# Attention with a fourth buffer for the stacks of keys, loads spread over the head steps, and a background list paced at 1.2 parts a step

## The chip, the cores and the metric

One core of a Trainium2 chip. The time is that of one execution on the device in microseconds (us); with one core its span is the program's. TensorE (PE) multiplies into PSUM, VectorE (DVE), ScalarE (ACT) and GpSimd (POOL) work on the results, and SyncE (SP) does nothing but issue transfers (DMAs). Every engine runs its own instructions in the order in which they were written, and waits at an instruction until what it depends on has been done.

## The reference

Two independent parts share the program. Part A is attention with 32 heads of 18 dimensions over a sequence of 2048, cut into 4 groups of 512 positions:

```python
for s in range(N):                       # N = 4 groups of L = 512 positions
    qs, ks, vs = q[:, :, s], k[:, :, s], v[:, :, s]
    p = softmax(einsum("bhqd,bhkd->bhqk", qs, ks) * scale + mask)   # causal inside the group
    a_dot = einsum("bhqk,bhkd->bhqd", p, vs)
    pq = phi(qs)                                                     # t+1 above zero, exp(t) below
    num = einsum("bhld,bhde->bhle", pq, M)
    den = einsum("bhld,bhd->bhl", pq, z)[..., None] + 1e-6
    outs.append(g * num / den + (1.0 - g) * a_dot)
    M = M + einsum("bhld,bhle->bhde", phi(ks), vs)
    z = z + einsum("bhld->bhd", phi(ks))
return (outs, heads side by side) @ wo
```

`M` and `z` are the memory of all earlier groups and `g` is a gate for each head. Part B multiplies the two-dimensional Fourier transform of another input of 2048 x 576 by given weights and transforms back.

## The kernel before

The program runs in four stages: forward transform of part B (to about 80 us), the projections q, k and v of part A with the middle of the transform beside them (to 287 us), the inverse transform with the first scores of attention beside it (to 377 us), and attention (377 to 882 us). The whole order is written out by hand: nothing is moved by a scheduler, so the order of the text is each engine's order. The change is in `ATT`, in what is issued from the third stage on.

**Stacks.** A stack is 8 heads of one group, so there are 16 (n = 0 to 15), 4 for each group. `stack_dmas` (L579) loads a stack's queries into `Qs[n%3]` and its keys into `Ks[n%3]` with six transfers each from `qkD` in device memory (three parts of bfloat16, stacked along the partitions in the pairs that the product needs), all issued by SP at L588; `load_v` (L594) brings the values. Rows 108 and 109 of a `Qs` hold the row maxima that `mpath` puts there; the same rows of a `Ks` hold -1.

**Head steps.** `attention` (L806) runs t = 0 to 132. A step's main work is `s1(t+10)`, the scores of a head ten steps on, of which DVE takes the row maxima (L603, L607; three parts); `s2(t)`, the scores of head t with the maxima taken off, ACT's exponentials and, every fourth head, POOL's four masks (L641 to L657; three parts); and `pv` (L668), the products with the values of four heads, one quarter a step. Every fourth step `mpath` turns the maxima of four heads (L622 on PE, L626 and L627 on ACT, L630 on DVE) and two transfers from POOL, `put(0)` and `put(1)` (L624), place them in `Qs`. `s1` of stack n starts at t = 8n-10.

**Queues.** At t = 8n the thirteen issues of stack n+2 are put on the list `q`. Two are taken in the middle of each step and up to two at its end, where the list `qu` (the results `U` of a stack, written back to `uD` and `rD`) comes first.

**Background list.** `bg` holds generators whose parts are run at the end of the steps, 1.6 parts a step on average (`run_bg(1.6)`, L864): `late_setup` (weights of the output product), and for each group `combine` (adds the memory's share to the attention), five `mem1` (the memory's numerators of the next group), `den` (its denominators) and `oproj` (the output product). They use one PSUM buffer, tag `post`: a product there can start only when the one before has been read out. The `lane` holds short chains such as `recip`, which advance once a step. `ln` starts at step 10 of a group (of 32 steps), and after `recip` it loads `ux` three times, waits three steps and hands `combine`, `mem1`, `den` and `oproj` to `bg`. In `mem1` the product `pn` (L735) and its copy `am` (L739) lie in two parts; in `oproj` the copy of one half of a block stands behind the first five products of the next half in the order of the text (`pend`), and each half of 15 products is three parts.

**Prologue.** During the inverse transform `prologue` loads stacks 0 and 1 and runs `s1` of the first ten heads.

Of the kernel before, what the change touches and what calls it, by code (L numbers as in the profile page):

```python
# [5 lines left out]
F32=mybir.dt.float32; F32R=mybir.dt.float32r  # L6
# [361 lines left out]
class ATT:  # L368
# [174 lines left out]
    def att_setup(s,cp):  # L543
        nc,io=s.nc,s.io
        s.Qs=[];s.Ks=[]
        for i in range(3):
            q=cp.tile([128,8,512],BF,name=f"Qs{i}"); k=cp.tile([128,8,512],BF,name=f"Ks{i}")
            s.Qs.append(q); s.Ks.append(k)
        for i in range(3): nc.gpsimd.dma_start(s.Ks[i][108:110].rearrange("p h c -> p (h c)"),io["neg1"])
        s.mask=cp.tile([128,512],F32,name="mask"); nc.sync.dma_start(s.mask,io["mask"])  # L550
        bt=cp.tile([128,1],F32,name="bt"); nc.sync.dma_start(bt,io["beta"])
        e=cp.tile([128,1],F32,name="be"); s.gt=cp.tile([128,1],F32,name="gt"); s.g1=cp.tile([128,1],F32,name="g1")
        nc.scalar.activation(e,bt,AF.Exp,scale=-1.0)
        nc.vector.tensor_scalar(e,e,1.0,None,op0=OP.add)
        nc.vector.reciprocal(s.gt,e)
        nc.vector.tensor_scalar(s.g1,s.gt,-1.0,1.0,op0=OP.mult,op1=OP.add)
        d=lambda n,sh,dt: s.dp.tile(sh,dt,name=n)
        s.uD=[d(f"uD{i}",[576,512],F32) for i in range(4)]
        s.rD=[d(f"rD{i}",[32,512],F32) for i in range(4)]
        s.dD=[None]+[d(f"dD{i}",[32,512],F32) for i in range(1,4)]  # L560
        s.rrD=[d(f"rrD{i}",[64,512],F32) for i in range(4)]
        s.rdD=[None]+[d(f"rdD{i}",[64,512],F32) for i in range(1,4)]

    def late_setup(s,cp):
# [13 lines left out]
        yield  # L578
    def stack_dmas(s,n):  # L579

        nc=s.nc; g,G=divmod(n,4)
        Q,K=s.Qs[n%3],s.Ks[n%3]
        L=[]
        for (T,base,order) in ((Q,0,(0,0,0,1,1,2)),(K,576,(0,1,2,0,1,0))):
            for pc,o in enumerate(order):
                a=s.qkD[g][base+8*G*18:base+8*G*18+18,o]
                ap=bass.AP(tensor=a.tensor,offset=a.offset,ap=[[1536,18],[1536*18,8],[1,512]])
                L.append(lambda T=T,pc=pc,ap=ap: nc.sync.dma_start(T[18*pc:18*pc+18],ap))  # L588
        L.append(lambda: s.loaded.add(n))
        return L  # L590
# [5 lines left out]
    def s1(s,t):  # L596

        nc=s.nc; k,hh=divmod(t,4); n,qd=divmod(k,2); h=4*qd+hh
        Q,K=s.Qs[n%3],s.Ks[n%3]; tp=s.sm
        assert n in s.loaded,(t,n)  # L600
        if hh==0: s.mg[k]=tp.tile([128,4,4],F32,name="mg")
        def mm(out,i):
            nc.tensor.matmul(out,Q[:108,h,128*i:128*i+128],K[:108,h,:128*(i+1)],start=True,stop=True)  # L603
        def red(src,i):
            w=128*(i+1)
            junk=tp.tile([128,512],BF,name="junk",bufs=2)
            nc.vector.tensor_tensor_reduce(out=junk[:,:w],in0=src,in1=s.mask[:,512-w:],scale=1.0,scalar=-3.0e38,  # L607
                op0=OP.add,op1=OP.max,accum_out=s.mg[k][:,hh,i:i+1])
        pa=s.ps1.tile([128,512],F32,name="s1",tag="s1")
        mm(pa[:,:128],0); mm(pa[:,128:],2); red(pa[:,:128],0); red(pa[:,128:],2)  # L610
        yield
        pc=s.ps1.tile([128,512],F32,name="s1",tag="s1")
        mm(pc,3); red(pc,3)
        yield
        pb=s.ps1.tile([128,256],F32,name="s1",tag="s1")
        mm(pb,1); red(pb,1)
        yield
    def mpath(s,k):
# [3 lines left out]
        nc.tensor.transpose(pt,s.mg.pop(k).rearrange("p h i -> p (h i)"),s.ident)  # L622
        mt=s.sm.tile([16,2,128],BF,name="mts")
        def put(a): nc.gpsimd.dma_start(Q[108+a:109+a,4*qd:4*qd+4].rearrange("p h (i c) -> p (h i) c",c=128),mt[:,a])  # L624
        mf=s.sm.tile([16,128],F32,name="mf")
        nc.scalar.copy(mf,pt)  # L626
# [6 lines left out]
    def s2(s,t):  # L633
        nc=s.nc; k,hh=divmod(t,4); n,qd=divmod(k,2); h=4*qd+hh
        Q,K=s.Qs[n%3],s.Ks[n%3]; tp=s.tp
        if hh==0: s.P[k]=[tp.tile([128,4,w],F32,name=f"P{i}") for i,w in enumerate((512,512,256))]
# [49 lines left out]
    def recip(s,src,dst,gate,eps,load):  # L686
        nc=s.nc; tp=s.tp
        x=tp.tile([128,128],F32,name="rx")
        nc.sync.dma_start(x,src.rearrange("h (b c) -> (h b) c",b=4))
# [3 lines left out]
        if eps: nc.vector.tensor_scalar(x,x,1e-6,None,op0=OP.add)  # L693
        y=tp.tile([128,128],F32,name="ry")
        nc.vector.reciprocal(y,x)
        nc.vector.tensor_scalar(y,y,gate,None,op0=OP.mult)
        w=tp.tile([128,2,128],F32R,name="rw")
        nc.vector.tensor_copy(w[:,0],y)
# [14 lines left out]
    def den(s,g,lane):  # L713
        nc=s.nc; tp=s.tp
        ds=tp.tile([128,512],F32,name="ds",bufs=1); ds2=tp.tile([32,512],F32,name="ds2",bufs=1)
        for T,d in ((range(4),ds),((4,),ds2)):
            pd=s.ps.tile([128,512],F32,name="pd",tag="post")
            for t in T:
                r=126 if t<4 else 72
                nc.tensor.matmul(pd[32*(t%4):32*(t%4)+32],s.zst[g][:r,t],s.pq[g,t][:r],start=True,stop=True,skip_group_check=True)  # L720
            yield
            nc.scalar.copy(d,pd[:d.shape[0]])
        for t in range(5):
# [8 lines left out]
    def mem1(s,g,t):  # L732
        nc=s.nc; r=126 if t<4 else 72
        pn=s.ps.tile([126,512],F32,name="pn",tag="post")
        nc.tensor.matmul(pn[:r],s.Mst[g][:r,t,:r],s.pq.pop((g,t))[:r],start=True,stop=True)  # L735
        if g<3: s.pq_load(g+1,t)
        yield
        am=s.tp.tile([126,512],F32,name="am",bufs=5)
        nc.scalar.copy(am[:r],pn[:r])  # L739
        pb=s.ps.tile([126,512],F32,name="pb",tag="post")  # L740
# [4 lines left out]
    def ux_load(s,g,t):  # L745
        r=126 if t<4 else 72
        s.ux[t]=s.tp.tile([126,512],F32,name="ux",bufs=3)
        s.nc.sync.dma_start(s.ux[t][:r],s.uD[g][126*t:126*t+r])
    def combine(s,g):

        nc=s.nc; tp=s.tp; xs=s.ux
        s.oh=[None]*5; s.ol=[None]*5
        for t in range(7):
            if t>1:
# [16 lines left out]
    def oproj(s,g):  # L771
        nc=s.nc; pend=None
        oh,ol=s.oh,s.ol
        for tb in range(4):
            ob=s.tp.tile([128,576],F32,name="ob")
            c=slice(128*tb,128*tb+128)
            for hf in range(2):
# [3 lines left out]
                for i,(a,b,t) in enumerate(L):  # L781
                    r=126 if t<4 else 72
                    nc.tensor.matmul(ps,a[t][:r,c],b[:r,t,w],start=i==0,stop=i==14)  # L783
                    if i==4 and pend: pend(); pend=None
                    if i%5==4: yield
                def pend(ob=ob,w=w,ps=ps,hf=hf,tb=tb):
                    nc.scalar.copy(ob[:,w],ps)  # L787
                    if hf==1: nc.sync.dma_start(s.io["ya"][g*512+128*tb:g*512+128*tb+128],ob)
        pend()
        yield  # L790
    def begin(s,sm,sp,ps1):
        s.sm,s.sp,s.ps1=sm,sp,ps1
        s.mg={};s.m2={};s.P={};s.vs={};s.rc={};s.am={};s.pq={};s.ux={};s.loaded=set()
    def prologue(s):

        for n in range(2):
            for i,f in enumerate(s.stack_dmas(n)):
                f()
                if i%4==3: yield
            s.load_v(n)  # L800
        for i in range(4): yield
        for t in range(10):
            yield from s.s1(t)
            if t in (4,8): m=s.mpath(t//4-1); next(m)
            if t in (5,9): next(m)
    def attention(s,tp,ps):  # L806
# [18 lines left out]
        for t in range(133):  # L825
            k,hh=divmod(t,4); n,qd=divmod(k,2); g=k//8
            if k<32 and hh==0 and qd==0 and n+2<16:
                q+=s.stack_dmas(n+2); q.append(lambda n=n: s.load_v(n+2))
            st=t%32
            if 16<=t<21: s.pq_load(1,t-16)  # L830
            if t==34: bg.append(s.den(1,lane))
            if st==10 and g>0:
                def ln(g=g):
                    yield from s.recip(s.rD[g-1],s.rrD[g-1],s.g1,False,"rr")
                    for u in range(3): s.ux_load(g-1,u)
                    for u in range(3): yield
                    bg.append(s.combine(g-1))
# [4 lines left out]
            a=s.s1(t+10) if t+10<128 else iter(())  # L842
            b=s.s2(t) if t<128 else iter(())
            steps(a,1)
            steps(b,1)
            steps(a,1)
            steps(b,1)
            if 4<=t-1<132: s.pv((t-5)//4,(t-5)%4)
            for _ in range(2):
                if q: q.pop(0)()  # L850
            steps(a,1)
            if hh==2 and k+2<32: m=s.mpath(k+2); next(m)
            steps(b,1)
            if hh==3 and m is not None: steps(m,1); m=None
            if t>=8 and t%4==0:
                s.pv_out((t-8)//4)
                if t%8==4: qu+=s.u_dmas((t-12)//8)
            for l in list(lane):
                try: next(l)
                except StopIteration: lane.remove(l)  # L860
            for _ in range(2):
                if qu: qu.pop(0)()
                elif q: q.pop(0)()
            run_bg(1.6)  # L864
        while q: q.pop(0)()
        while qu: qu.pop(0)()
        lane.append(s.recip(s.rD[3],s.rrD[3],s.g1,False,"rr"))
        while lane or bg:
            for l in list(lane):
                try: next(l)  # L870
                except StopIteration: lane.remove(l)
            run_bg(2.0)
        for u in range(3): s.ux_load(3,u)
        for _ in s.combine(3): pass
# [99 lines left out]
```

## Time and profile before

| what | value |
|---|---|
| median of three runs | 881.58 us (879.1 to 884.06) |
| profiled execution | 884.07 us |
| its span | 882.1 us, so 1.97 us lie around it |
| PE busy | 742.6 us (84%) |
| DVE busy | 584.8 us (66%) |
| ACT busy | 466.5 us (53%) |
| POOL busy | 182.5 us (21%) |
| DMA | 121.25 MB, 137 GB/s on the mean |
| granted clock of TensorE | 0.930 on the mean |

A line of the page's fifth part or of the waits names an engine, a line of the kernel and the operation; "idle before" is the time for which the engine stood still just ahead of such an instruction, and the arrow names what ended it. In a list in order of time the first two numbers are start and length in us; a number in brackets at the end is that idle time. "PEclk" is the share of full clock that was granted to TensorE, and "DMA" is the mean busy share of the core's 16 DMA engines.

### The profile page before, as it was taken

The page shows a single profiled execution, that of the slowest core. Times are in us where ns is not written, and L with a number is a line of the kernel's source. Part 1 is how long each engine was busy: PE and PEld are TensorE (multiplying, and loading weights), DVE is VectorE, ACT ScalarE, POOL GpSimd, SP SyncE. Part 2 cuts the span into 40 slices and gives each one's busy share as a digit, 9 for nine tenths or more (in the row PEclk, how much of TensorE's full clock was granted, in tenths as well). Part 3 has the DMA queues.
Part 4 walks back from the last instruction along what each step waited for, and adds up shares of the span by engine and source line. Part 5 has one row for each costly group of instructions (what it writes and reads, how often), then busy time and mean ns, then how long its engine had stood idle before and what let it go on. Part 6 is the DMA issues. An engine that isn't in the chain of part 4 may idle for free.

```text
span 882.1 us, 14645 instructions
## 1 busy us (share of the span) xinstructions
PE 742.6 (84%) x4751; PEld 495.3 (56%) x4751; DVE 584.8 (66%) x1687; ACT 466.5 (53%) x996; POOL 182.5 (21%) x339
## 2 busy tenths in 40 slices
PE   5988999999999699967777885888957798977856
PEld 4887797887979598922333331245512255422646
DVE  5998897977878799656665785546765565861040
ACT  3666966748565344346555664455644455664111
POOL 2110001010011644225332331122311121331000
PEclk9999999999999899978888998989977899989968
DMA  8873546445537685365654664534463345310121
GB/s 286 273 226 106 173 151 210 144 146 175 169 138 254 162 211 165 108 169 117 145 124 97 131 150 110 130 88 110 115 162 79 83 103 141 107 34 15 62 74 54
DMA packets 82463, 121.25 MB, mean 137 GB/s; under 512 B 9338, under 2 KB 49400, under 8 KB 82254
## 3 DMA queue, kind: packets, MB, share of 16 engines
q1 hardware_dynamic: 74836, 104.29, 42.3%
q0 software_dynamic: 7552, 16.03, 6.3%
q8 instruction: 38, 0.62, 0.3%
q14 instruction: 37, 0.30, 0.1%
HBM read 81.72 MB, written 38.35 MB: 136 GB/s over the span
## 4 chain that ended last, share of the span: by engine, by line
PE 57%; DMA 14%; DVE 11%; ACT 11%; issue 5%; POOL 1%; SPq 1%; ACTq 0%; DVEq 0%; POOLq 0%
PE pj L440 9%; PE po L783 8%; PE pv L668 8%; PE s L603 7%; PE pjv L440 7%; DMA Ks<-qkD 3%; DMA Qs<-qkD 3%; PE s L641 2%; DMA ux<-uD 2%; PE i L292 2%; PE i L303 2%; PE s L645 2%; PE pn L735 2%; DMA yb<-yout 2%; PE pm L497 1%
## 5 line engine op out<-in xcount | busy, mean ns | idle before, releaser
L607 DVE CUSTOM_DVE_ANT_0 junk<-s,mask 128x128 bf16<-128x128 f32 (+3 forms) x512 | 225.8, 485 | 118.0 <-PE s L603 116.2
L603 PE MATMUL s<-Ks,Qs 108*128 108x128 bf16 (+3 forms) x512 | 142.4, 323 | 27.4 <-DMA Ks<-qkD 10.5
L642 ACT ACTIVATE P<-s 128x512 f32<-128x512 f32 x128 | 76.4, 597 | 140.8 <-PE s L641 134.0
L603 PEld LDWEIGHTS <-Qs 108*128 108x128 bf16 x512 | 47.2, 102 | 130.0 <-issue 115.9
L668 PE MATMUL pv<-P,vs 128*32 128x512 f32 (+3 forms) x1024 | 104.8, 484 | 1.6 <-issue 1.1
L653 POOL TENSOR_SCALAR_AFFINE_SELECT P<-P 128x512 f32<-128x512 f32 x128 | 81.0, 663 | 50.9 <-ACT P L642 49.3
L624 POOL DMA_DIRECT2D Qs<-mts x64 | 31.7, 495 | 273.1 <-ACT P L651 229.3
L647 ACT ACTIVATE P<-s 128x512 f32<-128x512 f32 x128 | 76.0, 594 | 4.1 <-PE s L646 4.1
L440 PE MATMUL pj<-xh,wqkh 128*128 128x512 f32 x180 | 71.2, 395 | 0.5 <-ACT Z L151 0.5
L440 PE MATMUL pj<-xh,wqkl 128*128 128x512 f32 x180 | 71.1, 395 | 0.0
L651 ACT ACTIVATE P<-s 128x256 f32<-128x256 f32 x128 | 48.3, 377 | 31.1 <-PE s L650 30.1
L440 PE MATMUL pj<-xl,wqkh 128*128 128x512 f32 x144 | 61.8, 429 | 0.0
L641 PE MATMUL s<-Qs,Ks 110*128 110x512 bf16 x128 | 53.6, 418 | 6.5 <-DMA Qs<-mts 3.2
L202 DVE TENSOR_TENSOR Z<-t,t 128x290 f32<-128x290 f32 (+1 forms) x96 | 52.9, 596 | 0.2
L292 PE MATMUL i<-civ,Y 128*128 128x256 f32 (+1 forms) x288 | 44.5, 309 | 8.3 <-DVE T L320 4.6
L783 PE MATMUL po<-woh,oh 126*128 126x288 f32 (+1 forms) x160 | 32.7, 337 | 19.7 <-ACT ob L787 17.4
L202 DVE TENSOR_TENSOR t<-Z 128x580 f32<-128x580 f32 x64 | 48.0, 788 | 0.2
L440 PE MATMUL pjv<-wvh,xh 128*128 128x288 f32 x160 | 48.1, 303 | 0.0
L440 PE MATMUL pjv<-wvl,xh 128*128 128x288 f32 x160 | 46.2, 295 | 0.0
L292 PEld LDWEIGHTS i<-civ,Y 128*128 128x128 f32 (+1 forms) x288 | 39.8, 199 | 10.7 <-DVE T L320 5.9
L645 PE MATMUL s<-Qs,Ks 110*128 110x384 bf16 x128 | 45.3, 354 | 0.0
L607 DVE DVE_READ_ACCUMULATOR2_ANT mg<- 128x1 f32 x512 | 41.2, 80 | 0.0
(140 smaller groups left out, 1507.7 us busy)
## 6 DMA issues: line engine op xcount, KB each, us to landing
qkD<-sp SPq DMA_DIRECT2D x36, 384.0 KB
Qs<-qkD SPq DMA_DIRECT2D x96, 144.0 KB
Ks<-qkD SPq DMA_DIRECT2D x96, 144.0 KB
xin<-xb SPq DMA_DIRECT2D x16, 384.0 KB
cfw<-cfw POOLq DMA_DIRECT2D x16, 384.0 KB, 4.4
civ<-civ POOLq DMA_DIRECT2D x16, 384.0 KB, 6.9
vs<-vD SPq DMA_DIRECT2D x16, 330.0 KB
vD<-vt SPq DMA_DIRECT2D x16, 311.0 KB
```

The source lines that it names most:

```text
L202: v.tensor_tensor(o,a,b,op=op)
L292: nc.tensor.matmul(p[:m,k],Y[i][:,q,c*128:c*128+m],cc[:,hl,o:o+256],start=n==0,stop=n==5)
L440: s.nc.tensor.matmul(out,a,b,start=i==0,stop=i==len(L)-1)
L603: nc.tensor.matmul(out,Q[:108,h,128*i:128*i+128],K[:108,h,:128*(i+1)],start=True,stop=True)
L607: nc.vector.tensor_tensor_reduce(out=junk[:,:w],in0=src,in1=s.mask[:,512-w:],scale=1.0,scalar=-3.0e38, op0=OP.add,op1=OP.max,accum_out=s.m ...
L641: nc.tensor.matmul(p0,kk(0),q(0),start=True,stop=True)
L642: nc.scalar.activation(P[0][:,hh],p0,AF.Exp,scale=SC)
L645: nc.tensor.matmul(p1[:,:384],kk(1),q(128),start=True,stop=True)
L647: nc.scalar.activation(P[1][:,hh],p1,AF.Exp,scale=SC)
L653: sel=lambda x,pat: nc.gpsimd.affine_select(out=x,in_=x,pattern=pat+[[1,128]],compare_op=OP.is_ge,fill=0.0,base=0,channel_multiplier=-1)
L668: nc.tensor.matmul(s.pvt[32*hh:32*hh+32,128*j:],vt[:,j,19*h:19*h+32],mv[0][:,hh,mv[1]],start=jj==0,stop=jj==3,skip_group_check=True)
L783: nc.tensor.matmul(ps,a[t][:r,c],b[:r,t,w],start=i==0,stop=i==14)
```

## The change

- There are four `Ks` buffers instead of three. The keys of stack n+3 and the queries of stack n+2 are now put on `q` at t = 8n; the keys of stack 2 are loaded in the prologue, one issue for each part of `s1`. `stack_dmas` makes the list for queries or keys alone.
- `q` and `qu` each give one issue at the start and one at the end of a step.
- `mpath` has one more stop, behind the transpose: `mf`, `mts` and `put(0)` come behind the third part of `s2` of that step, and DVE's difference with `put(1)` comes ahead of the third part of `s1` of the next step, no longer behind its `s2`.
- `den`, `mem1` and `oproj` read a product into SBUF directly behind it, in the same part. `oproj` has two parts a half (8 and 7 products) instead of three.
- The rate of the background list is 1.2 parts a step instead of 1.6 (1.0 instead of 2.0 behind the last step). `combine` loads `ux` itself and has two empty parts behind that, and `ln` no longer waits three steps.
- `junk`, `mts`, `mf`, `rx`, `ry` and `rw` have one buffer instead of two, and `ds` and `ds2` share the three buffers of `ux`.

```diff
@@ att_setup
-        for i in range(3):
-            q=cp.tile([128,8,512],BF,name=f"Qs{i}"); k=cp.tile([128,8,512],BF,name=f"Ks{i}")
-            s.Qs.append(q); s.Ks.append(k)
+        s.Qs=[cp.tile([128,8,512],BF,name=f"Qs{i}") for i in range(3)]
+        s.Ks=[cp.tile([128,8,512],BF,name=f"Ks{i}") for i in range(4)]
@@ stack_dmas
-    def stack_dmas(s,n):
+    def stack_dmas(s,n,qk):
...
-        for (T,base,order) in ((Q,0,(0,0,0,1,1,2)),(K,576,(0,1,2,0,1,0))):
...
+        T,base,order=((s.Qs[n%3],0,(0,0,0,1,1,2)),(s.Ks[n%4],576,(0,1,2,0,1,0)))[qk]
@@ s1
-            junk=tp.tile([128,512],BF,name="junk",bufs=2)
+            junk=tp.tile([128,512],BF,name="junk",bufs=1)
@@ mpath
-        mt=s.sm.tile([16,2,128],BF,name="mts")
+        mt=s.sm.tile([16,2,128],BF,name="mts",bufs=1)
         def put(a): nc.gpsimd.dma_start(Q[108+a:109+a,4*qd:4*qd+4].rearrange("p h (i c) -> p (h i) c",c=128),mt[:,a])
-        mf=s.sm.tile([16,128],F32,name="mf")
+        yield
+        mf=s.sm.tile([16,128],F32,name="mf",bufs=1)
         nc.scalar.copy(mf,pt)
@@ den
-        ds=tp.tile([128,512],F32,name="ds",bufs=1); ds2=tp.tile([32,512],F32,name="ds2",bufs=1)
+        ds,ds2=[tp.tile([128,512],F32,name=f"ds{i}",tag="ux",bufs=3) for i in range(2)]; ds2=ds2[:32]
...
+            nc.scalar.copy(d,pd[:d.shape[0]])
             yield
-            nc.scalar.copy(d,pd[:d.shape[0]])
@@ mem1
-        if g<3: s.pq_load(g+1,t)
-        yield
         am=s.tp.tile([126,512],F32,name="am",bufs=5)
         nc.scalar.copy(am[:r],pn[:r])
+        if g<3: s.pq_load(g+1,t)
+        yield
@@ combine
+        for u in range(3): s.ux_load(g,u)
+        yield
+        yield
         for t in range(7):
@@ oproj
-                    if i==4 and pend: pend(); pend=None
-                    if i%5==4: yield
-                def pend(ob=ob,w=w,ps=ps,hf=hf,tb=tb):
-                    nc.scalar.copy(ob[:,w],ps)
-                    if hf==1: nc.sync.dma_start(s.io["ya"][g*512+128*tb:g*512+128*tb+128],ob)
-        pend()
-        yield
+                    if i==7: yield
+                nc.scalar.copy(ob[:,w],ps)
+                if hf==1: nc.sync.dma_start(s.io["ya"][g*512+128*tb:g*512+128*tb+128],ob)
+                yield
@@ prologue
-            for i,f in enumerate(s.stack_dmas(n)):
+            for i,f in enumerate(s.stack_dmas(n,0)+s.stack_dmas(n,1)):
...
+        q=s.stack_dmas(2,1)
         for t in range(10):
-            yield from s.s1(t)
+            for _ in s.s1(t):
+                if q: q.pop(0)()
+                yield
@@ attention
-            if k<32 and hh==0 and qd==0 and n+2<16:
-                q+=s.stack_dmas(n+2); q.append(lambda n=n: s.load_v(n+2))
+            if hh==0 and qd==0:
+                if n+2<16: q+=s.stack_dmas(n+2,0)
+                if n+3<16: q+=s.stack_dmas(n+3,1)
+                if n+2<16: q.append(lambda n=n: s.load_v(n+2))
...
-                    for u in range(3): s.ux_load(g-1,u)
-                    for u in range(3): yield
                     bg.append(s.combine(g-1))
...
+            if q: q.pop(0)()
+            if qu: qu.pop(0)()
             steps(a,1)
             steps(b,1)
             steps(a,1)
             steps(b,1)
             if 4<=t-1<132: s.pv((t-5)//4,(t-5)%4)
-            for _ in range(2):
-                if q: q.pop(0)()
+            if hh==3 and m is not None: steps(m,1); m=None
             steps(a,1)
             if hh==2 and k+2<32: m=s.mpath(k+2); next(m)
             steps(b,1)
-            if hh==3 and m is not None: steps(m,1); m=None
+            if hh==2 and m is not None: steps(m,1)
...
-            for _ in range(2):
-                if qu: qu.pop(0)()
-                elif q: q.pop(0)()
-            run_bg(1.6)
+            if q: q.pop(0)()
+            if qu: qu.pop(0)()
+            run_bg(1.2)
```

## The prediction

> **What bounds the kernel now.** I first read the busy table in 40 slices: up to the 17th slice (375 us) PE is nearly full, behind it it is at 7 or 8 tenths, and nothing else is full there either. So the change, which touches attention alone (377 to 882 us), has room where PE stands still. Next the waits of PE in the loop of head steps, 377 to 828 us (what it waited for: us in total, times, longest):
>
> ```profile
> PE pb L741 <- ACT am L739: 16.1, 15, 1.8
> PE po L783 <- ACT ob L787: 11.8, 17, 1.0
> PE pb L762 <- DVE ux L767: 11.3, 5, 6.0
> PE s L603 <- DMA Ks<-qkD: 10.5, 2, 5.3
> PE pb L762 <- DVE am L765: 7.7, 2, 6.8
> PE s L603 <- DMA pq<-pqD: 5.1, 1, 5.1
> PE s L603 <- DMA uD<-U: 4.5, 2, 3.8
> PE pn L735 <- DVE am L742: 3.9, 5, 0.8
> PE pd L720 <- ACT ds L722: 3.3, 3, 1.3
> PE s L641 <- DMA Qs<-mts: 3.2, 3, 1.3
> ...
> PE pd L720 <- DVE am L742: 1.6, 2, 0.8
> ```
>
> Three kinds are seen: `s1` waiting for its stack (L603: the transfer named is the last by the profile, but all stand at the first head of a stack), the background products waiting for the one PSUM buffer `post` to be read (L741, L783, L735, L720), and `combine` waiting for `ux` or DVE (L762). Then PE in order of time, around a border of stacks and where nothing disturbs it:
>
> ```profile
> 395.41 0.59 PE L603 MATMUL s<-Ks,Qs 108*128 108x128 bf16 x2 [5.17 <-DMA Ks<-qkD]
> 395.79 0.63 PE L641 MATMUL s<-Qs,Ks 110*128 110x512 bf16 x1
> ...
> 405.46 0.38 PE L603 MATMUL s<-Ks,Qs 108*128 108x128 bf16 x2
> 405.68 0.38 PE L641 MATMUL s<-Qs,Ks 110*128 110x512 bf16 x1
> ...
> 407.56 0.38 PE L603 MATMUL s<-Ks,Qs 108*128 108x128 bf16 x2
> ...
> 763.36 0.64 PE L668 MATMUL pv<-P,vs 128*32 128x256 f32 x8
> ...
> 771.91 0.64 PE L668 MATMUL pv<-P,vs 128*32 128x256 f32 x8
> ```
>
> After 5.17 us of standing still the same product takes 0.63 us instead of 0.38: the clock is lower, and that step lasts 3.85 us (395.41 to 399.26) where the like one at 405.46 lasts 2.10. A stall over 3.7 us so costs another 1.75. From 763.36 to 771.91 lie four undisturbed steps: 2.14 us each, the step's price on PE. DVE's four maxima take 1.64 us a step (402.28 to 403.92) and ACT's three exponentials 1.57 (597, 594 and 377 ns), so PE is the bound where nobody waits. Last, windows while stack loads are queued (the last two numbers of a row are the DMA share and GB/s), and one in `combine`:
>
> ```profile
> 381.00:386.00 5.00, 5.00 (x21) 2.65 (x20) 3.96 (x17) 3.79 (x9) 0.51 (x2) 0.50 0.73 163
> 386.00:390.00 4.00, 3.77 (x28) 1.58 (x25) 3.91 (x19) 3.67 (x8) 3.77 (x6) 0.99 0.81 195
> ...
> 427.00:433.00 6.00, 5.82 (x49) 2.50 (x49) 5.15 (x25) 4.67 (x12) 1.62 (x4) 1.00 0.72 176
> ...
> 757.00:777.00 20.00, 17.87 (x133) 8.09 (x132) 18.90 (x70) 12.95 (x31) 7.22 (x12) 0.96 0.33 99
> ```
>
> With 390.00 to 395.40 (159 GB/s) and 411.50 to 415.00 (172) the loads of stacks run at 172 GB/s on the mean, weighted by length.
>
> **The change part by part.** The sum is made against the profiled execution (884.07 us); the median was 2.5 us lower.
>
> *Loads (four `Ks`, even issue).* Now all twelve pieces of a stack, 12 x 144 KB, are asked for at t = 8n to 8n+3 and needed at 8n+6; the last landed 10.0, 9.1 and 10.0 us after its issue in the chain of waits. The keys get eight more steps, and the six pieces of queries go out two a step, 0.29 MB in 2.14 us, or 135 GB/s, under the 172; the last is out by 8n+3, three steps or 6.4 us early. Waits to be had: 24.3 us (10.5, 5.1 and 4.5, and 2.3 and 1.9 of the same list for rD<-U and DVE rw), the 3.2 for `Qs<-mts`, and the clock behind four long stalls, 4 x 1.75 = 7.0: together 34.5. But from 376 to 472 us (t = 0 to 31) the DMA moved 132 GB/s x 96 us = 12.7 MB, at 172 GB/s 74 us, while PE needs 32 x 2.14 = 68. So that stage can fall from 96 to 74 and no further, 22 us; with 4 us at the later borders and 2 us kept back for pieces that still come late, **-24** (bounds -10 and -34.5). A page speaks against more: the Trainium skill, "DMA: Bandwidth & Descriptors", section on why a DMA increments its semaphore by 16, says that a copy issued from SP uses the largest number of engines up to 16 that divides the slowest dimension of both sides, which for the 18 rows of a piece is 9. By it spreading would raise no rate; the shares of 0.72 to 0.81 above are short of full, as it would have it, but other transfers ran beside.
>
> The vs load, thirteenth on the list, held SP for 49.5 us in nine waits from 477 us on, as its buffer is read to step 8n+4; it now comes at 8n+6 and waits for nothing. What `mpath` moves: ACT's two copies (254 and 297 ns) come behind an exponential and DVE's difference (469 ns) ahead of one maximum; `put(1)` goes ahead of the four masks (663 ns each) in POOL's queue. Masks now stand behind `put(1)`, which waits for DVE, but they need the last exponential of that step, which is later. Nothing; if DVE were late, the first mask would be, and with it `pv`. The single buffers cost nothing, as each is written again four or more steps after its last reader; `junk` is written by DVE alone, in order.
>
> *`mem1`.* The copy now follows `pn` at once, and `pb` comes a step later with the buffer free: 16.1 + 3.9 = 20.0 us go. At 1.2 parts a step every sixth part shares its step with another: 30 parts, 5 pairs at 1.07 (16.1/15) or 0.78 (3.9/5), 4.7. **-15** (-8 to -20).
>
> *`oproj`.* The 11.8 us for `ob` go, 0.69 each; of 38 parts inside the loop 6 share a step and half of these meet a copy, 2.2. **-9.5** (-4 to -11.8). Behind the loop the halves follow each other as now.
>
> *`den`.* 3.3 + 1.6 = 4.9 go, 1.5 pairs at 1.2 stay. **-3** (0 to -4.9).
>
> *`combine`.* 19.0 us of waits. Three of them, 6.8, 6.0 and 2.4 us, are for `ux`, which lay behind a burst of stack loads; with even loads they land in the two empty parts. But DVE has 0.68 + 0.75 + 0.69 = 2.1 us for each of five pieces beside 1.64 a step, at 1.2 pieces 4.2 us against PE's 2.14 + 0.7, and was at 18.90 of 20 us in the window above. I take half back: **-8** (0 to -19).
>
> *Pace.* A group has 9 + 10 + 3 + 16 = 38 parts (`combine`, `mem1`, `den`, `oproj`), 31.7 steps of 32 at 1.2: it just fits. From step 112 to 132 25 of 35 parts are done, so ten, five halves of `oproj`, come behind the loop, where now thirteen of 25 do, 4.3 halves. The products are only moved: nothing, and there they cover the chain of `recip(3)`, as now.
>
> *ACT behind the products.* A copy written straight behind its product makes ACT wait for it ahead of the next step's exponential, and 15 + 6 + 19 copies do. PE goes on meanwhile: the next exponential's input is ready 0.44 us after the product (0.22 + 0.22, the pace at 405.46), and the copy ends 0.59 after it. 40 x 0.15 = **+6** (0 to 40 x 0.44 = +18).
>
> *Prologue.* Six more loads (0.86 MB, 5.0 us at 172 GB/s) between the yb stores. The store at 320.14 took 10.95 us in the chain, and DVE waited 0.7 us and PE 0.9 for it. **+1.5** (0 to +5).
>
> Sum: -24 - 15 - 9.5 - 3 - 8 + 6 + 1.5 = -52. 884.07 - 52 = 832 as a profiled execution, 881.58 - 52 = **830 us** as a median.
>
> **The rivals.** *The transfers themselves are the bound from t = 0 to 31.* For it: 74 us at the best rate seen, with PE at 68, and by the page's nine engines no better can be had; against: 96 us are taken now, and keys may lag eight steps. Loads then bring 5 instead of 24, and the time is 881.6 - 33 = 849.
>
> *The background waits come back.* There is one buffer `post`, so a product waits for the last one's reader wherever ACT or DVE lags a whole step. For it: ACT at 87% of the undisturbed window from 400 to 413 us; against: 2.1 us lie between two parts. With 15, 9.5, 3 and 8 us not had and the +6 left out: 881.6 - 24 + 1.5 = 859.
>
> *Slower: queries late at every border.* Queries go out two pieces a step, each in SP's order behind `U`, `ob` and `ya` stores that wait for ACT. If the last lands over three steps (6.4 us) behind its issue, `s1` stops at all 14 borders (stacks 2 to 15) and not at some: 14 x (5.2 + 1.75) = 97 instead of 34.5, +63, less the -28 of the other parts: 881.6 + 35 = 917. For it: landings of 9 to 10 us today; against: those lay behind eleven pieces, these behind two or three.
>
> **How the numbers follow.** Forecast 0.78, transfers 0.08, background 0.06, late queries 0.08. Half of what lies between the sum and the bounds (-90 and +1) is taken on each side, rounded outward: 808 to 860 holds the first three, and late queries lie outside. About 0.5% (4.4 us) is what a measurement of this kernel can tell from no change: 0.02 of the forecast and 0.01 each of background and late queries end inside it. Faster 0.76 + 0.08 + 0.05 = 0.89, the same 0.04, slower 0.07.
>
> **What would show it.** At the first head of each stack the L603 waits for transfers should go from 24.3 us to under 6, t = 0 to 31 should take about 76 us, L741's wait for `am` should fall from 16.1 to about 4 and L783's for `ob` in the loop from 11.8 to about 2. DMA share in the first four stacks should rise to 0.7 and the step be PE's. It is wrong if L603 still waits 4 us or more at most borders, if ACT's wait for L735, L720 and L783 delays L642 so that PE waits at L641, or if the inverse transform ends after 382 us.

## The result and the profile after

The changed kernel takes 823.94 us as the median of four runs (820.21 to 829.64), the kernel before beside it 882.48; the ratio is 0.9347 (95% interval 0.9284 to 0.9410). 58.5 us are won; 52 were forecast. A median here is over all executions of a kernel, while a ratio leaves out those more than 1.5% longer than the kernel's fastest. The profiled execution has a span of 818.2 us against 882.1.

PE's waits in the loop of head steps, 370 to 770 us (what it waited for: us in total, times, longest), to be held against the list of before:

```profile
PE s L602 <- DVE mg L606: 15.5, 40, 1.6
PE mt L621 <- DVE mg L606: 10.2, 8, 2.9
PE pb L765 <- DVE ux L770: 3.8, 2, 2.6
PE s L641 <- ACT P L642: 2.8, 2, 1.8
PE pn L735 <- DVE am L742: 2.5, 2, 1.7
PE pb L741 <- ACT am L737: 1.6, 2, 0.9
PE pb L765 <- DVE am L768: 1.5, 2, 1.2
PE pd L720 <- DVE am L742: 1.3, 1, 1.3
PE po L786 <- ACT ob L788: 1.0, 2, 0.5
...
PE s L602 <- DMA Ks<-qkD: 0.3, 1, 0.3
```

The waits for loads are gone (0.3 us where it was 24.3), and those of `mem1`, `oproj` and `den` for the `post` buffer nearly so (6.4 us where it was 36.7). What is new stands on top: PE now waits 25.7 us for DVE's maxima (`mg`), where it was 3.2. The chain of the work that ended last, over the whole span, says the same; before, it had DMA at 14% and DVE at 11%:

```profile
PE 60%; DVE 21%; ACT 8%; issue 6%; DMA 3%; SPq 1%; POOL 0%; DVEq 0%; ACTq 0%
```

The first stacks, once as a window (span, busy us of PE, PE's weight loads, DVE, ACT and POOL, granted clock, DMA share, GB/s):

```profile
376.00:455.00 79.00, 67.42 (x478) 26.80 (x479) 64.38 (x261) 55.75 (x122) 31.73 (x49) 0.96 0.65 158
```

and DVE in order of time inside them (start, length, engine, line, operation):

```profile
417.09 0.29 DVE L606 CUSTOM_DVE_ANT_0 junk<-s,mask 128x128 bf16<-128x128 f32 x1
417.31 0.08 DVE L606 DVE_READ_ACCUMULATOR2_ANT mg<- 128x1 f32 x1
417.43 0.56 DVE L606 CUSTOM_DVE_ANT_0 junk<-s,mask 128x384 bf16<-128x384 f32 x1
417.91 0.08 DVE L606 DVE_READ_ACCUMULATOR2_ANT mg<- 128x1 f32 x1
418.14 0.69 DVE L606 CUSTOM_DVE_ANT_0 junk<-s,mask 128x512 bf16<-128x512 f32 x1
418.75 0.08 DVE L606 DVE_READ_ACCUMULATOR2_ANT mg<- 128x1 f32 x1
418.98 0.42 DVE L606 CUSTOM_DVE_ANT_0 junk<-s,mask 128x256 bf16<-128x256 f32 x1
419.33 0.08 DVE L606 DVE_READ_ACCUMULATOR2_ANT mg<- 128x1 f32 x1
419.56 0.29 DVE L606 CUSTOM_DVE_ANT_0 junk<-s,mask 128x128 bf16<-128x128 f32 x1
```

In the kernel before a step reads:

```profile
402.28 0.27 DVE L607 CUSTOM_DVE_ANT_0 junk<-s,mask 128x128 bf16<-128x128 f32 x1
402.49 0.07 DVE L607 DVE_READ_ACCUMULATOR2_ANT mg<- 128x1 f32 x1
402.49 0.54 DVE L607 CUSTOM_DVE_ANT_0 junk<-s,mask 128x384 bf16<-128x384 f32 x1
...
403.92 0.07 DVE L607 DVE_READ_ACCUMULATOR2_ANT mg<- 128x1 f32 x1
```

The busy lengths are those of before, within 0.02 us. But each maximum starts later behind the start of the accumulator reading ahead of it than it did: 417.31 to 417.43, 417.91 to 418.14, 418.75 to 418.98, 419.33 to 419.56, that is 0.12 and three times 0.23 us. In the kernel before, the next maximum and that reading start at the same time. A head step is now 2.47 us of DVE (417.09 to 419.56) instead of 1.64 (402.28 to 403.92), more than the 2.14 that PE needs: DVE sets the pace.

### The profile page after: what moved, and what is told of

It is laid out like the page before. It is cut to its first block, busy times and chain, and to the rows that moved or that the text cites. A ratio compares the mean times of both kernels' runs of the same rounds, so it can differ in the third digit from the quotient of the medians.

```text
span 818.2 us, 14656 instructions
## 1 busy us (share of the span) xinstructions
PE 727.3 (89%) x4751; PEld 489.2 (60%) x4751; DVE 611.9 (75%) x1687; ACT 472.3 (58%) x996; POOL 181.0 (22%) x340
## 4 chain that ended last, share of the span: by engine, by line
PE 60%; DVE 21%; ACT 8%; issue 6%; DMA 3%; SPq 1%; POOL 0%; DVEq 0%; ACTq 0%
PE pj L440 10%; PE po L786 8%; DVE junk L606 8%; PE s L602 8%; PE pv L668 7%; PE pjv L440 7%; PE i L292 3%; PE i L303 3%; PE s L641 2%; PE s L645 2%; PE pn L735 2%; PE pm L497 1%; DMA Qs<-qkD 1%; PE s L650 1%; DVE eo L123 1%
## 5 line engine op out<-in xcount | busy, mean ns | idle before, releaser
L606 DVE CUSTOM_DVE_ANT_0 junk<-s,mask 128x128 bf16<-128x128 f32 (+3 forms) x512 | 251.3, 491 | 71.6 <-PE s L602 27.1
L602 PE MATMUL s<-Ks,Qs 108*128 108x128 bf16 (+3 forms) x512 | 138.2, 313 | 19.5 <-DVE mg L606 16.2
L602 PEld LDWEIGHTS <-Qs 108*128 108x128 bf16 x512 | 47.1, 100 | 114.4 <-issue 100.9
L668 PE MATMUL pv<-P,vs 128*32 128x512 f32 (+3 forms) x1024 | 100.0, 463 | 1.0 <-issue 0.8
L653 POOL TENSOR_SCALAR_AFFINE_SELECT P<-P 128x512 f32<-128x512 f32 x128 | 77.0, 641 | 14.2 <-ACT P L642 13.8
L641 PE MATMUL s<-Qs,Ks 110*128 110x512 bf16 x128 | 51.2, 400 | 3.6 <-ACT P L642 2.8
L645 PE MATMUL s<-Qs,Ks 110*128 110x384 bf16 x128 | 43.5, 340 | 0.1
L788 ACT COPY ob<-po 128x288 f32<-128x288 f32 x32 | 12.7, 398 | 48.3 <-PE po L786 48.1
```

Of the source, the lines that this page charges most:

```text
L641: nc.tensor.matmul(p0,kk(0),q(0),start=True,stop=True)
L645: nc.tensor.matmul(p1[:,:384],kk(1),q(128),start=True,stop=True)
L653: sel=lambda x,pat: nc.gpsimd.affine_select(out=x,in_=x,pattern=pat+[[1,128]],compare_op=OP.is_ge,fill=0.0,base=0,channel_multiplier=-1)
L668: nc.tensor.matmul(s.pvt[32*hh:32*hh+32,128*j:],vt[:,j,19*h:19*h+32],mv[0][:,hh,mv[1]],start=jj==0,stop=jj==3,skip_group_check=True)
```

## The experiments

Theory O: the gaps come from `junk`, which the change cut from two buffers to one, so that each maximum waits for the write of the one before it. Its rivals are that the transfers set the pace now (T) and that PE does (N). The second pair of experiments does each half of the change alone.

**Two junk buffers in the changed kernel.**

```diff
-            junk=tp.tile([128,512],BF,name="junk",bufs=1)
+            junk=tp.tile([128,512],BF,name="junk",bufs=2)
@@ recip
-        x=tp.tile([128,128],F32,name="rx",bufs=1)
+        w=tp.tile([128,2,128],F32R,name="rw",bufs=1)
+        x=y=w[:,1].bitcast(F32)
...
```

`recip` now works in place in `rw`, only to make room for the second buffer.

> The changed kernel with two junk buffers again; room comes from recip working in place in rw. Theory O (with one junk buffer each of DVE's maxima waits for the write of the one before it; in the changed kernel they start 0.11 to 0.23 us apart from the end of the last, a step of DVE takes 2.46 us and not 1.64, and DVE sets the step): the step from t = 5 to 32 falls from 2.48 us to 2.15 to 2.25, PE's waits for mg fall from 25.7 us (15.5 at s1, 10.2 at the transposes) to under 8, and the time from 824 to 800 to 810. Rival T (the transfers bound the first four stacks, at 172 GB/s 74 us for t = 0 to 31, where the changed kernel takes 79): waits move to the stack loads, at most 5 us are won, 818 to 822. Rival N (junk does not matter, PE sets the step): 821 to 827.

806.03 us, ratio 0.9097 (0.9044 to 0.9150). DVE in order of time:

```profile
412.58 0.28 DVE L606 CUSTOM_DVE_ANT_0 junk<-s,mask 128x128 bf16<-128x128 f32 x1
412.79 0.07 DVE L606 DVE_READ_ACCUMULATOR2_ANT mg<- 128x1 f32 x1
412.79 0.54 DVE L606 CUSTOM_DVE_ANT_0 junk<-s,mask 128x384 bf16<-128x384 f32 x1
...
414.22 0.07 DVE L606 DVE_READ_ACCUMULATOR2_ANT mg<- 128x1 f32 x1
414.22 0.27 DVE L606 CUSTOM_DVE_ANT_0 junk<-s,mask 128x128 bf16<-128x128 f32 x1
```

The gaps are gone and a step of DVE is 1.64 us again. The one cut buffer costs the change 17.9 us by the medians (823.94 - 806.03). From the products with the values of step 5 to those of step 32 the kernel before takes 84.7 us, the changed kernel 67.0 and this one 63.2, or 2.34 a step and not the 2.15 to 2.25 of theory O. PE's waits in the loop (377 to 750 us) show why:

```profile
PE mt L621 <- DVE mg L606: 6.4, 5, 2.5
PE s L602 <- DVE mg L606: 5.2, 9, 1.1
...
PE s L602 <- DMA pq<-pqD: 3.7, 1, 3.7
...
PE s L602 <- DMA Ks<-qkD: 2.1, 2, 1.4
```

Those for DVE fell from 25.7 to 11.6 us, not under 8, and 5.8 us for loads came back at three borders of the first four stacks. In these stacks (376 to 452 us) the waits for the maxima are down to 0.3 us; beside the loads 3.7 us are left for ACT at L641. Theory O holds in its cause and in the time, not in its step and its waits, and behind DVE loads are waited for again, as T has it.

**One junk buffer in the kernel before.** The edit is the same line the other way, alone.

> The kernel before with junk in one buffer, nothing else changed. Theory O: undisturbed steps go from 2.14 to about 2.46 us and the maxima show the same gaps of 0.11 to 0.23 us; in the first four stacks the waits for loads hide most of it, so 888 to 900 against 882. Rival N: the same within 3 us, 879 to 885.

893.1 us, or 891.7 without the longest execution, ratio 1.009 (1.0047 to 1.0133): theory O from the other side, with the buffer as the only edit. The gaps stand there too, and so does the wait, which was 1.6 us:

```profile
406.21 0.29 DVE L607 CUSTOM_DVE_ANT_0 junk<-s,mask 128x128 bf16<-128x128 f32 x1
406.43 0.08 DVE L607 DVE_READ_ACCUMULATOR2_ANT mg<- 128x1 f32 x1
406.54 0.56 DVE L607 CUSTOM_DVE_ANT_0 junk<-s,mask 128x384 bf16<-128x384 f32 x1
```
```profile
PE s L603 <- DVE mg L607: 12.4, 34, 1.1
```

Four steps without a wait for a load, from 428.38 to 437.95 us, last 2.39 us each; theory O had 2.46. The same cut cost some 8 us here (891.7 against 883.63) and 17.9 in the changed kernel. The expectation's reason, that waits for loads hide the rest, fits, as PE still stands 14.7 us for loads at `s1` there, but no run tests it.

**The loads alone, and the background part alone,** each put into the kernel before, with two junk buffers. The edits are the parts of the change's diff that belong to each; for room the first also has `ds` and `ds2` in the buffers of `ux`, single `mts` and `mf`, and `recip` in place. Both keep the old `mpath`.

> The kernel before with the loads of the change alone: four Ks, keys a stack earlier, one issue of each list at the start and at the end of a step, keys of stack 2 in the prologue; junk keeps two buffers (room: recip in place, single mts and mf, ds and ds2 in the buffers of ux). The background list is as before, at 1.6 parts. The prediction's terms: -24 and +1.5, so 860 (850 to 872). Rival T: -5, so 877. If combine's long waits for ux were the burst of stack loads, they go here already and the time is 845 to 853.

853.9 us, ratio 0.9636 (0.9566 to 0.9706). PE's waits (377 to 800 us), without one at `s1` for a load:

```profile
PE pb L739 <- ACT am L737: 16.0, 15, 1.6
PE po L781 <- ACT ob L785: 13.3, 20, 1.0
PE pb L760 <- DVE ux L765: 5.7, 4, 2.4
...
PE pb L760 <- DMA ux<-uD: 4.3, 1, 4.3
```

> The kernel before with the background part of the change alone: products read straight behind, oproj in two parts a half, 1.2 parts a step, combine loading ux itself. Loads, three Ks, junk in two buffers and mpath as before. The prediction's terms: -15, -9.5, -3, -8 and +6, so 853 (843 to 863). If combine's long waits are due to the loads, they stay and it is 861. Rival of the background waits coming back: 875 to 885.

843.71 us; without the two longest of its four executions 837.1 (835.30 and 838.92), on which the ratio of 0.9452 (0.9366 to 0.9539) rests. Its profile is that of the longest (850.32 us), so its waits are read for their kinds and only roughly for their size: those for loads at `s1` are all there (two kinds are shown), those of the background list are nearly gone.

```profile
PE s L603 <- DMA Ks<-qkD: 9.7, 2, 4.8
PE s L603 <- DMA pq<-pqD: 9.6, 3, 5.4
...
PE pb L765 <- DVE ux L770: 1.9, 1, 1.9
...
PE pb L741 <- ACT am L737: 1.6, 2, 0.9
```

The loads bring 29.7 us and the background part 46.5 (883.63 against 837.1; 39.9 by the median of all four), each more than the 22.5 and 29.5 of the prediction. With the loads alone the steps from 5 to 32 fall from 84.7 to 63.6 us, and `combine`'s waits from 19.0 to 10.9: 21.1 and 8.1, which is nearly all of the 29.7. With the background part alone those steps still take 82.7 us; `combine`'s waits fall to 4.9, and those of `mem1`, `oproj` and `den` from 36.7 to some 6. Both halves shorten `combine`'s waits, yet the two sum to 76.2 and both together, with two junk buffers, bring 77.6. So within the scatter of the runs the halves add up.

**The pace.** This and all further kernels start from the changed kernel with two junk buffers (806.0 us).

```diff
-            run_bg(1.2)
+            run_bg(1.6)
```

> The changed kernel with two junk buffers (806.0 us, the base of this and the next three) and the background list at 1.6 parts a step instead of 1.2; products still read straight behind. Theory P (a product waits for the reader of the one before it only where two parts share a step): three steps in five have two parts, of 30 parts of mem1 some 11 pairs at 0.93 and of 38 of oproj some 14 pairs, half of them at 0.69, so PE's waits at the pn, pb and po lines go from 5.7 us to about 18 and the time to 814 to 820. Rival S (reading straight behind is enough, the pace does nothing, as the list ends sooner and PE has the same work): 803 to 809.

823.28 us, ratio 0.9354 (0.9277 to 0.9431), slower than either theory expected. PE's waits from 370 to 840 us, loop and tail together:

```profile
PE pb L764 <- DMA rr<-rrD: 10.0, 1, 10.0
...
PE po L785 <- ACT ob L787: 6.6, 13, 0.5
...
PE pb L740 <- ACT am L736: 4.0, 6, 0.7
PE pn L734 <- DVE am L741: 3.9, 5, 0.8
```

Pairs cost what theory P said only in part: in the loop alone the waits of `mem1` and `oproj` for `am` (on ACT and on DVE) and `ob` are 9.9 us where the base has 3.7, a rise of 6.2 (it had expected one of some 12), and `combine`'s at its `pb` rise from 6.8 to 13.6. The largest single piece is one wait behind the loop: at 1.6 parts `oproj` of group 2 is done inside the loop, and the last `recip` (its load, the reciprocals, a store and the load of `rr`) then runs with PE standing still for 10.0 us. In the base, where 1.2 leaves ten parts behind the loop, no such wait stands in the list.

**Three `Ks` buffers, even issue.**

```diff
-        s.Ks=[cp.tile([128,8,512],BF,name=f"Ks{i}") for i in range(4)]
+        s.Ks=[cp.tile([128,8,512],BF,name=f"Ks{i}") for i in range(3)]
...
-                if n+3<16: q+=s.stack_dmas(n+3,1)
+                if n+2<16: q+=s.stack_dmas(n+2,1)
```

The index of `Ks` becomes `n%3`, and the prologue no longer loads the keys of stack 2.

> The base with three Ks buffers: keys and queries of stack n+2 both from t = 8n, in that order reversed (queries first), one issue at the start and one at the end of a step; nothing is loaded ahead in the prologue. Theory K (the fourth buffer is what lets the loads be even): the last piece of keys goes out at step 8n+5 and is needed at 8n+6, so s1 waits 2 to 4 us at most of the 14 borders, 840 to 860. Rival E (the even issue alone does it): 805 to 812.

887.24 us, ratio 1.006 (1.0009 to 1.0111), far past both. PE waits at the first head of a stack at all 14 borders, 2.1 to 8.9 us each, 70.6 in all; the transfer named is the last by the profile:

```profile
PE s L602 <- DMA rD<-U: 22.5, 4, 8.3
PE s L602 <- DMA vs<-vD: 20.9, 4, 7.9
...
PE s L602 <- DMA Ks<-qkD: 8.0, 2, 4.6
```

Even issue without the lead of the keys takes back all that the change brings. This is the picture of the prediction's slower rival, a last piece that is late at every border, with the keys in the place of the queries, as they are issued last here. The fourth buffer keeps it out: the keys are long there, and the queries go first.

**Four `Ks`, the old burst.**

```diff
-            if q: q.pop(0)()
-            if qu: qu.pop(0)()
             steps(a,1)
...
+            for _ in range(2):
+                if q: q.pop(0)()
...
+            for _ in range(2):
+                if qu: qu.pop(0)()
+                elif q: q.pop(0)()
```

> The base with four Ks and the issue as in the kernel before: two from the list of loads in the middle of a step, and up to two at its end where the results do not come first. Theory K (only the lead of the keys counts): the six pieces of queries go out first in any case, 803 to 810. Rival B (bursts hold up ux, results and pq, and through them combine): combine's waits at the pb line go from 12 us to 20 or more, 814 to 825.

819.26 us, ratio 0.9307 (0.9246 to 0.9368): rival B's time, but not through `combine`'s waits at `pb`, which rise from 13.5 to 14.2 us only, over the whole loop and the tail. What grew is the transpose's wait for DVE, from 6.4 to 15.8 us. At the longest of them, 5.8 us, DVE stood at the reciprocal for `rD`, and the maxima queued behind it: SP issued that load at 485.31 us, behind ten loads of the burst and 3.5 us of waiting for the store of `rw`, its own buffer; in the base it issued it at 476.37. At the next, 4.3 us, DVE stood for 4.2 us ahead of a product of `combine` with `ux`; what ended that wait the profile does not name.

```profile
490.46 0.95 DVE L695 RECIPROCAL rw<-rw 128x128 f32<-128x128 f32 x1 [4.86 <-DMA rw<-rD]
```
```profile
PE mt L621 <- DVE mg L606: 15.8, 6, 5.8
...
PE s L602 <- DMA Ks<-qkD: 5.2, 2, 4.9
```

**The loads of `pq` spread.**

```diff
-            if 16<=t<21: s.pq_load(1,t-16)
+            if t in (12,16,20,24,28): s.pq_load(1,(t-12)//4)
```

> The base with the five loads of pq (1.15 MB, needed at step 34) at t = 12, 16, 20, 24 and 28 instead of 16 to 20. Theory T (with DVE's gaps gone the transfers are the next limit in the first four stacks, fullest at t = 16 to 22, where PE waited 3.7 us for the queries of stack 4 behind the loads of pq): that wait falls under 1 us and the time to 800 to 804. If the transfers bind over all of t = 0 to 31, the wait moves to another border and the time stays at 804 to 808.

809.01 us, ratio 0.9200 (0.9143 to 0.9258): nothing won, and neither case of the expectation came true. The wait stays at the same border, 3.3 us where it was 3.7, now put down to the queries themselves. So that `pq` was issued at t = 16 to 20 was not its cause. Windows of base and variant over the first stacks (376 to 450 us) move 163 and 159 GB/s at a DMA share of 0.71, near the 172 seen while loads were queued before. That fits transfers bounding the stage, but does not show it; which of them would have to go was not tried.

**The old `mpath`.** The two stops and the order of the kernel before, in the base.

> The changed kernel with two junk buffers (806.0 us), mpath as in the kernel before: ACT's two copies ahead of the third exponential, DVE's difference and put(1) behind the third part of s2 of the next step and so behind POOL's four masks. The prediction set the move of mpath at nothing: 803 to 809, with waits for Qs<-mts at most 2 us. Rival M (put(1) behind 2.4 us of masks lands too late at the denser steps: 2.14 us now where they averaged 3.1 in the kernel before): PE waits 1 to 2 us for Qs<-mts at many of the 30 places, 815 to 835.

804.71 us, ratio 0.9122 (0.9078 to 0.9167), with no wait for `Qs<-mts` in the list: the move of `mpath` costs and brings nothing that the median shows. The trace does show a difference. With the old order PE waits 8.2 us in five places at the third part of `s2` (L649), where ACT has its two copies ahead of the exponential, and the base has no such row. In exchange the waits for loads fall from 5.8 to 0.5 us. The steps from 5 to 32 take 65.8 us against 63.2, and six executions scatter from 798.26 to 810.04, so what the move is worth stays open.

**`ux` earlier in the tail.**

```diff
+        c=s.combine(3); early=True
         while lane or bg:
...
+            if early: next(c); early=False
             run_bg(1.0)
-        for _ in s.combine(3): pass
+        for _ in c: pass
```

> The changed kernel with two junk buffers, and the first three loads of ux of the last combine issued right behind the load of the last recip, while oproj of the group before still runs, and not behind all of its stores. In the base these loads go out at 762.0 us, when PE has nothing else, and PE waits 3.7 us for the first. They need nothing that is late: 802 to 803. Rival (SP then waits at them for the last results' stores and holds up recip's chain): 806 to 810.

804.19 us, ratio 0.9120 (0.9090 to 0.9151). The first loads go out at 754.3 us instead of 762.0 and PE no longer waits 3.7 us for them (0.5, for a copy), but the median is no further from the base than the runs scatter, and lies between the two that were expected: open. It, the kernel before it and the base all beat the changed one by 18 to 20 us.

## Why the prediction was right

The forecast (830, range 808 to 860) and its main case held: PE's waits for loads and for `post` went. But a wait that the sum put at nothing, for DVE's maxima, grew from 3.2 to 25.7 us, and that the sum still came near is luck.

- *Loads, -24:* right in mechanism. Alone with the prologue's part they brought 29.7 us instead of 22.5, and not the 5 of the transfers rival. The L602 wait fell to 0.3 us where under 6 was forecast. In t = 5 to 32 they were worth 21.1 us alone, where the term had 22 for the stage, and the mean granted clock of the stage rose from 0.82 (376 to 472 us) to 0.96 (376 to 455). As changed the stage takes some 79 us where about 76 was expected, as DVE set the step. With two junk buffers it takes some 74, the floor of the prediction. That transfers make this floor is not shown: the kernel with the loads alone (63.6 us for steps 5 to 32, no wait for a load at `s1`) and that with `pq` spread (62.8) lie at the same length with other waits. How many engines a piece is spread over, on which the transfers rival drew, no run shows. The two expected signs that DMA share would rise to 0.7 and the step be PE's failed as changed (0.65, and DVE's); with two junk buffers the share is 0.71.
- *`mem1`, `oproj`, `den`, -27.5:* the waits fell from 20.0 to 4.1, 11.8 to 1.0 and 4.9 to 1.3, or 30.3 us. Pairs of parts met a reader less often than one in six.
- *`combine`, -8:* under-sized. The waits fell from 19.0 to 5.3 us. The even loads alone brought them to 10.9 and the background part alone to 4.9. How much of the latter is the two empty parts and how much the pace was not taken apart.
- *ACT behind the products, +6:* wrong. PE's wait for ACT at L641 is 2.8 us, and was 2.5: the copies hide. With two junk buffers it is 4.6, of which 3.7 lie in the first four stacks.
- *Prologue, +1.5:* nothing seen; `s2` starts at 376.58 us, and did at 376.48.
- *The single buffers, 0:* the step that failed. "`junk` is written by DVE alone, in order" is true, and does not make it free: with one buffer the next maximum still came later, 0.8 us a step, and 17.9 us of the time. That the sum came out near is two misses of opposite sign: some 24 us more were won than reckoned (58.5 and 17.9 against 52), and 18 were lost here.

## What to carry to other kernels

A buffer that nobody reads can still set the pace: before cutting its count, look whether the engine that writes it does so back to back, as the cost is then a wait ahead of each instruction. Lead and even issue belong together: loads spread over the steps needed one buffer more here, or the last piece was late at every border. And a background list that is short of done when the loop ends can be worth more than one that is finished, where the last chain of transfers needs cover.

## What the runs showed of the hardware

With one buffer for an output that is written over by the next instruction of the same engine, DVE's maxima start 0.12 to 0.23 us later each. Against the recorded end of the maximum before, they start 0.05 to 0.16 us behind it with one buffer (417.38 to 417.43 is the shortest gap), and 0.06 to 0.07 us ahead of it with two (412.79 against 412.86). That the number of buffers makes it is shown, in both kernels and both directions; that it is a wait for the end of the engine's own write is the reading. The Trainium skill, "VectorE: DVE Perf Modes", section on the DRAIN that can't be avoided, reports eight copies taking the same time with a semaphore behind each as with one behind the last, and says that the semaphore costs nothing extra there. Whether those copies wrote one buffer it does not say, so it is not the same test. In these runs what comes with the single buffer costs 0.8 us a step of four maxima (0.12 + 3 x 0.23).
